# Grouped-query attention with a gated MLP on one core: next batch's transposes, the score lead, PSUM bank choice and the last batch rearranged

## The chip, the cores and the metric

One core of one Trainium2 chip. The time is device microseconds (us) of one execution, the median over runs (4 to 11 of a kernel). A profile's span is about 2 us shorter than the time of the same run.

Names: PE is TensorE (its matmuls), PEld its weight loads, ACT ScalarE, DVE VectorE, POOL GpSimd, SP SyncE (here it only issues DMAs; SPq is its queue).

Tiles in the profile lines: `sc` scores, `aT` their exps, `sums` and `X` the value products, `rec` one over the sums, `xt` the normalised X, `pv` and `v_r` the V half of the MLP, `rstd` one over its standard deviation, `v_n` V normalised, `psp` and `v_s` the spatial product, `pu` the U half, `gT` the gated product, `po` and `osb` an output tile.

## The reference, cut to what matters

Eight batches, 384 tokens. 16 query heads and 4 key/value heads of width 64 (each k/v head serves 4 query heads), then a gated MLP whose gate mixes over tokens.

```python
scores = q @ k.T / 8                        # per head, 384 x 384
attn   = exp(scores - max) / (sum + 1e-9)
x      = concat over heads of attn @ v       # (8, 384, 1024)
h      = relu(x @ w_in)                     # 1024 -> 1024
u, v   = h[..., :512], h[..., 512:]
v_n    = (v - mean) / sqrt(var + 1e-6)      # over the 512
v_s    = w_spatial @ v_n + b_spatial        # mixes the 384 tokens
out    = (u * v_s) @ w_out                  # 512 -> 1024, fp32
```

## The kernel before: the parts that matter

The kernel keeps three batches in flight. While batch `b` runs its value products (`value`: the sums of exps and two halves of X, 36 matmuls of 32-column tiles), its predecessor `c = b-1` runs the gated MLP and `d = b-2` its output. Between these blocks `more(n)` computes scores of a *later* batch, one unit (two row-tile matmuls and one exp over 128x1024) at a time, from one running list. The schedule is written by hand: each engine is given its instructions in exactly the order in which the code below emits them.

Many products are split by rows: rows 0 to 63 and rows 64 to 127 of the array work on different PSUM banks at once (`LO`, `HI`), and in a second pass they swap banks. Between the passes stands a join: a tiny memset (`mark` on POOL, `mark_v` on DVE) that waits for the first pass and that the second pass waits for.

The Trainium skill, "PSUM — Partial Sum Buffer", section "PSUM bank collisions raise a hardware error", quotes the reason for joins: different row tiles must not access the same PSUM bank at the same time.

```python
turn = [0]
def bank(shape, dtype, name, i=None):
    if i is None:
        i = turn[0]
    turn[0] = (i + 1) % 4
    return ps.tile(shape, dtype, name=name, tag=f"ps{i}")

def more(n):
    for _ in range(n):
        bu = next(ahead, None)
        if bu is not None:
            score_mm(*bu)
            exp(*bu)

def group_sp(b, banks):
    done = {}
    for m in (0, 2):
        last = pairs(sp_part(b, m, LO, banks[m]), sp_part(b, m + 1, HI, banks[m + 1]))
        done[m] = passed(last)
        if m == 0:
            more(1)
    for m in (0, 2):
        pairs(sp_part(b, m + 1, LO), sp_part(b, m, HI), after=done[m])
        sp_add(b, m)
        sp_add(b, m + 1)
        if m == 0:
            more(1)

def group_vo(bv, st, bo, i0, i1, banks, counts=(0, 2, 0), relu_on=None, then=None):
    lo = [*v_part(bv, st, LO, banks[0])]
    hi = [*o_part(bo, i0, HI, banks[1])], [*o_part(bo, i1, HI, banks[2])]
    hi = [*hi[0][:2], *hi[1][:2], *hi[0][2:], *hi[1][2:]]
    last = pairs(lo, hi, {4: [lambda: more(counts[0])]})
    done = passed(last, nc.vector)
    if then is not None:
        then()
    more(counts[1])
    pairs(
        [*o_part(bo, i0, LO), *o_part(bo, i1, LO)],
        v_part(bv, st, HI),
        {4: [lambda: o_copy(bo, i0), lambda: more(counts[2])]},
        after=done,
    )
    relu(bv, st, relu_on)
    o_copy(bo, i1)
    stats(bv, st)

def batch(b, f, o0, v, o1, late):
    c, d = b - 1, b - 2
    nxt = b + 1 < B
    value(b, 0, (f, o0, v))
    more(1)
    xmul(b, 0)
    if nxt:
        cast_all_k(b + 1)
        cast_all_q(b + 1, 0)
    group_vo(c, 2, d, 2, 3, (o1, f, o0), (late, 2, 0), nc.vector)
    if nxt:
        cast_all_q(b + 1, 1)
        cast_v(b + 1, nc.gpsimd)
        dma_transposes(b + 1)
    f, o0, v, o1 = v, f, o1, o0
    value(b, 1, (f, o0, v))
    more(1)
    rstd(c)
    xmul(b, 1)
    norm(c, 0, 2)
    group_vo(b, 0, d, 4, 5, (o1, f, o0), (late, 2, 0), then=lambda: norm(c, 2, 3))
    if b + 2 < B:
        load_all(b + 2)
    f, o0, v, o1 = v, f, o1, o0
    more(1)
    group_sp(c, (f, o0, v, o1))
    if late:
        more(1)
        group_u(c, (f, o0, v, o1))
        value(b, 2, (f, o0, v))
        more(1)
        xmul(b, 2)
    else:
        value(b, 2, (f, o0, v))
        more(1)
        xmul(b, 2)
        group_u(c, (o1, f, o0, v))
        more(2)
    if nxt:
        group_vo(b, 1, c, 0, 1, (o1, f, o0), (late, 2, late), nc.vector)
        more(1)
    return v, f, o1, o0
# (cut: loads, casts, first and second batch, tail)
```

`dma_transposes(b+1)` puts three DMA transposes (k, and q in two parts, fp16 copies made by POOL) into the SP queue. `o_copy` copies an output tile on DVE and puts its store into the same SP queue.

The softmax here doesn't subtract the row's maximum and nothing guards it: scores larger than these inputs give would overflow.

## Time and profile before

| | before |
|---|---|
| time, median | 269.22 us |
| span of the profile | 267.1 us |
| PE busy | 244.1 us, 91% |
| ACT, DVE, POOL busy | 68%, 55%, 18% |
| period of a middle batch (start of the first sums of batch 4 to that of batch 5: 128.08 to 158.19) | 30.11 us |

The page's busy line and its summary of the chain that ended last say which engine bounds the kernel:

```profile
PE 244.1 (91%) x2549; PEld 119.0 (45%) x2549; DVE 148.2 (55%) x289; ACT 181.9 (68%) x225; POOL 47.1 (18%) x100
...
PE 70%; ACT 10%; DMA 8%; DVE 6%; SPq 3%; issue 1%; ACTq 0%
```

PE bounds it, so only gaps of PE can be won. A step of 512 columns occupies 0.215 us from one start to the next (seen below); the Trainium skill, "TensorE: Matmul & The Clock Gate", section "Back-to-back issue gap", gives N/2.4 + 2.5 ns for an isolated matmul, which is 216 ns for 512 columns, and about 131 ns for a sustained stream; the trace agrees with the first and not with the second, for the sixteen full-height matmuls of two V blocks in the tail take 3.46 us in a row (241.83 to 245.29), 0.216 each. A start-to-start distance above that is lost time. The list of waits (engine, line, what it waited for, then: us in total, times, longest) names the two waits that matter:

```profile
PEld L540 <- DVE mark_v L585: 4.9, 10, 0.7
PE sc L286 <- ACT aT L297: 4.2, 11, 0.7
PE sc L286 <- DMA qT<-q: 4.1, 4, 1.6
DVE v_n L380 <- ACT rstd L373: 3.6, 7, 0.6
```

**The wait for qT.** The timeline of PE in batch 4 (start, duration, engine, line, what, in brackets the idle time ahead and its releaser):

```profile
141.26 0.38 PE L500 MATMUL pv<-w_in,xt 64*128 64x512 f16 x1
142.55 0.39 PE L286 MATMUL sc<-qT,kT 64*128 64x512 f16 x2 [0.92 <-DMA qT<-q]
```

A pair starts 0.215 us after the pair ahead of it; here 1.29 us pass from the last pair at 141.26 to the score at 142.55, so 1.1 us are lost. Over batches 3 to 6 such gaps make 4.7 us. The SP queue of the same batch shows why the data came so late:

```profile
129.29 7.17 SPq L464 DMA_DIRECT2D out_dram<-osb  x2
136.59 1.36 SPq L221 DMA_TRANSPOSE kT<-k  x1
138.07 3.35 SPq L228 DMA_TRANSPOSE qT<-q  x2
```

The row of 7.17 us merges two output stores, the second of which waits for a DVE copy until 136.1. POOL's casts, the input of the transposes, had been ready since 125.6. The first half of q landed at 142.42, and the score that needs it started at 142.55.

**The join that is late.** ACT and DVE around the group with the third output tile, same batch:

```profile
137.17 1.02 ACT L297 ACTIVATE aT<-sc 128x1024 f16<-128x1024 f32 x1 [0.35 <-PE sc L286]
138.09 0.29 ACT L372 ACTIVATE rstd<-mv,eps_t 128x3 f32<-128x3 f32 x1
138.41 0.20 ACT L373 ACTIVATE rstd<-rstd 128x3 f32<-128x3 f32 x1
```

```profile
136.86 1.29 DVE L334 TENSOR_TENSOR xt<-X,rec 128x512 f16<-128x512 f32 x2
138.65 1.47 DVE L380 TENSOR_SCALAR v_n<-v_r,mv,rstd 128x512 f16<-128x512 f32 x3 [0.50 <-ACT rstd L373]
139.59 0.06 DVE L585 MEMSET mark_v<- 1x1 f32 x1
```

The join memset at 139.59 stands behind two `v_n` on DVE, these wait for `rstd` on ACT, and `rstd` stands behind an exp. On PE, the four score matmuls ahead of the join are worth two steps, 0.43 us, but 1.03 us pass until the second pass starts:

```profile
138.70 0.79 PE L286 MATMUL sc<-qT,kT 64*128 64x512 f16 x4
139.73 0.39 PE L540 MATMUL po<-w_out,gT 64*128 64x512 f16 x1 [0.25 <-DVE mark_v L585]
```

So PE loses 0.60 us at this join, and 0.10 us at the sister group's.

**Stages.** Durations of single profiles are compared below by three stages that leave out the start-up (whose length alone varies by up to 1.5 us from profile to profile: the second sums of batch 1 start between 47.8 and 49.3 us). A: from the second sums of batch 1 to those of batch 2. B: from there to the second sums of batch 7. C: from there to the first U matmul of the tail (tile `sc_u`). All are starts read from the PE timeline of one profile for each kernel.

### The profile page before, as it was taken

Reading aid. Unit: us, or ns where it says so; the run is one execution under the profiler, and the core shown is the slowest. Engines: PE = TensorE matmul, PEld = TensorE weight load, DVE = VectorE, ACT = ScalarE, POOL = GpSimd, SP = SyncE. Lnnn points to the kernel's source line nnn. Section 1 sums busy time; section 2 is a strip of 40 time slices with the busy share of each in tenths; the row PEclk is TensorE's granted clock in tenths of the full one; section 3 lists DMA queues with packets and bytes.
Section 4 is the critical chain, followed back from the end, with each engine's and each line's share of the span. In section 5 each row is a group of like instructions: output and inputs, shape, how many; then the busy total and the mean of one; then the engine's idle time right before and its main releaser. Section 6 shows DMA issues by size and latency. Waiting matters only on the chain.

```text
span 267.1 us, 6034 instructions
## 1 busy us (share of the span) xinstructions
PE 244.1 (91%) x2549; PEld 119.0 (45%) x2549; DVE 148.2 (55%) x289; ACT 181.9 (68%) x225; POOL 47.1 (18%) x100
## 2 busy tenths in 40 slices
PE   2887988998999999799998999899999999999993
PEld 1233433553346534355444544355444544454551
DVE  2326666544276456653686356753687356757452
ACT  2889768969878696687777786687778696510501
POOL 2707803024000610007000430007000000000000
PEclk9999999999999999999999999999999999999998
DMA  8999996992269711993259801994247001210506
GB/s 185 280 260 350 271 201 85 154 312 64 81 167 277 218 66 60 198 313 107 81 137 258 267 7 77 219 320 121 81 129 179 0 20 72 103 49 0 236 2 236
DMA packets 57579, 41.68 MB, mean 156 GB/s; under 512 B 26832, under 2 KB 53840, under 8 KB 57552
## 3 DMA queue, kind: packets, MB, share of 16 engines
q1 hardware_dynamic: 53648, 37.75, 52.0%
q0 software_dynamic: 2720, 3.15, 8.4%
q10 hardware_dynamic: 1184, 0.39, 0.6%
q8 instruction: 20, 0.33, 0.5%
q14 instruction: 7, 0.06, 0.1%
HBM read 25.95 MB, written 12.58 MB: 144 GB/s over the span
## 4 chain that ended last, share of the span: by engine, by line
PE 70%; ACT 10%; DMA 8%; DVE 6%; SPq 3%; issue 1%; ACTq 0%
PE pu L513 14%; PE po L540 10%; PE sc L286 10%; PE X L307 8%; ACT aT L297 8%; DMA qT<-q 6%; PE pv L500 6%; PE sums L307 5%; PE pv L346 5%; PE psp L526 4%; PE po L442 4%; SPq L221 2%; DVE v_s L406 2%; DMA q<-in_q_dram 1%; PE pu L416 1%; DVE v_r L358 1%
## 5 line engine op out<-in xcount | busy, mean ns | idle before, releaser
L297 ACT ACTIVATE aT<-sc 128x1024 f16<-128x1024 f32 x144 | 141.0, 1023 | 41.4 <-PE sc L286 41.2
L540 PE MATMUL po<-w_out,gT 64*128 64x512 f16 x288 | 69.0, 376 | 1.7 <-DVE mark_v L585 1.2
L286 PE MATMUL sc<-qT,kT 64*128 64x512 f16 x288 | 57.1, 392 | 9.7 <-ACT aT L297 4.2
L500 PE MATMUL pv<-w_in,xt 64*128 64x512 f16 x272 | 65.8, 377 | 0.0
L513 PE MATMUL pu<-xt,w_in 64*128 64x384 f16 x448 | 41.3, 323 | 0.2 <-DVE v_s L406 0.2
L459 DVE COPY osb<-po 128x512 f32<-128x512 f32 x39 | 26.8, 689 | 22.9 <-PE po L540 19.4
L334 DVE TENSOR_TENSOR xt<-X,rec 128x512 f16<-128x512 f32 x48 | 30.9, 686 | 11.1 <-ACT rec L326 8.9
L307 PE MATMUL X<-aT,v 128*32 128x512 f16 x576 | 35.9, 384 | 0.0
L540 PEld LDWEIGHTS <-gT 64*128 64x128 f16 x288 | 25.5, 94 | 20.2 <-DVE mark_v L585 4.9
L286 PEld LDWEIGHTS <-kT 64*128 64x128 f16 x288 | 17.5, 94 | 37.3 <-issue 27.2
L428 DVE SCALAR_TENSOR_TENSOR gT<-pu,v_s 128x384 f16<-128x384 f32 x31 | 16.0, 553 | 27.4 <-PE pu L513 26.0
L513 PEld LDWEIGHTS <-w_in 64*128 64x128 f16 x448 | 24.1, 94 | 14.5 <-issue 1.4
L587 POOL MEMSET mark<- 1x1 f32 x28 | 2.5, 89 | 158.6 <-PE psp L526 116.4
L500 PEld LDWEIGHTS <-xt 64*128 64x128 f16 x272 | 24.4, 94 | 12.4 <-issue 5.5
L168 POOL CAST q<-q 128x768 f16<-128x768 f32 (+2 forms) x32 | 23.5, 770 | 27.1 <-DMA q<-in_q_dram 19.9
L406 DVE TENSOR_TENSOR v_s<-psp,bias_b 128x384 f32<-128x384 f32 x32 | 19.9, 685 | 11.2 <-PE psp L526 7.9
L307 PEld LDWEIGHTS <-v 128*32 128x32 f16 x576 | 16.5, 98 | 15.5 <-issue 1.3
L325 ACT ACTIVATE rec<-sums 128x512 f32<-128x512 f32 x24 | 14.5, 603 | 11.4 <-PE sums L307 11.4
L307 PE MATMUL sums<-aT,ones 128*32 128x512 f16 x288 | 20.6, 392 | 0.5 <-DVE v_s L406 0.3
L526 PE MATMUL psp<-wsT,v_n 64*128 64x384 f16 x168 | 17.6, 322 | 0.2 <-ACT v_r L360 0.2
L358 DVE TENSOR_SCALAR v_r<-pv 128x512 f32<-128x512 f32 x18 | 12.5, 692 | 9.0 <-PE pv L346 6.3
L367 DVE BATCH_NORM_STATS2 stats<-v_r 128x6 f32<-128x512 f32 x24 | 16.5, 690 | 0.2
(56 smaller groups left out, 154.6 us busy)
## 6 DMA issues: line engine op xcount, KB each, us to landing
out_dram<-osb SPq DMA_DIRECT2D x23, 512.0 KB, 2.9
q<-in_q_dram SPq DMA_DIRECT2D x14, 768.0 KB, 8.3
v<-in_v_dram SPq DMA_DIRECT2D x8, 384.0 KB, 8.7
k<-in_k_dram SPq DMA_DIRECT2D x7, 384.0 KB, 4.4
w_in<-in_moe_w_in_dram POOLq DMA_DIRECT2D x8, 256.0 KB, 8.9
q<-in_q_dram SPq DMA_DIRECT2D x2, 512.0 KB, 6.2
w_out<-in_moe_w_out_dram POOLq DMA_DIRECT2D x2, 512.0 KB, 20.9
ws<-in_moe_w_spatial_dram SPq DMA_DIRECT2D x1, 576.0 KB, 9.6
```

The source lines that it names most:

```text
L168: engine.tensor_copy(dst, src)
L286: mm = nc.tensor.matmul(sc[:, half, :], kT[b][lo:hi, gp, t, :], rhs[lo:hi, :], start=True, stop=True)
L297: nc.scalar.activation(aT[b, qt][:, gp, t], held["sc", b, u], AF.Exp, scale=scale)
L307: nc.tensor.matmul(dst[32 * g : 32 * (g + 1), :], weights(t, g), a[:, g // 2, t, g % 2, :], start=(t == 0), stop=(t == NST - 1),)
L334: nc.vector.tensor_tensor(xt[:, jj, :, qt * P : (qt + 1) * P], held["X", b, qt, jj].rearrange("p (j q) -> p j q", j=G), held["rec", b, qt] ...
L367: nc.vector.bn_stats(s6, held["v_r", b, st])
L406: nc.vector.tensor_tensor(held["v_s", b][:, m, :].rearrange("p (t s) -> p t s", t=NST), held["psp", b, m][:, 0:S].rearrange("p (t s) -> p ...
L459: nc.vector.tensor_copy(osb[:, cols], held["po", b, i])
L500: yield lambda kc=kc: nc.tensor.matmul(held["pv", b, st], xT[b][rows, kc, st * P : (st + 1) * P], w_in16[rows, kc, DH:DFF], start=(first a ...
L513: yield lambda kc=kc: nc.tensor.matmul(held["pu", b, mu][:, 0:S], w_in16[rows, kc, mu * P : (mu + 1) * P], xT[b][rows, kc, :], start=(firs ...
L526: yield lambda st=st: nc.tensor.matmul(held["psp", b, m][:, 0:S], held["v_n", b, st][rows, m * P : (m + 1) * P], wsT16[rows, st, :], start ...
L540: yield lambda m=m: nc.tensor.matmul(held["po", b, i], held["gT", b][rows, m, tt * P : (tt + 1) * P], w_out16[rows, m, half * 512 : (half ...
```

## The change

Its intent: (a) cast and transpose the next batch's q and k at the head of a batch, ahead of the output stores; (b) let the scores run one unit less ahead, so that the transposed data is wanted later; (c) put `rstd` ahead of the exp; (d) choose PSUM banks by least recent use; (e) in the last batch, where no scores are left to interleave, use full-height matmuls without joins for the spatial product and U, and do one V block earlier. The start of the diff (the `bank` function: a list in order of last use in place of a turning counter; default banks `None` in the groups) is cut; this is the rest:

```diff
@@ -775,24 +776,23 @@
         norm(0)
         v_full(1, 0)
         more(2)
-        group_sp(0, (0, 1, 2, 3))
+        group_sp(0)
         dma_transposes(2)
         more(1)
-        value(1, 1, (0, 1, 2))
+        value(1, 1)
         more(1)
         xmul(1, 1)
         load_all(3)
-        group_u(0, (3, 0, 1, 2))
-        more(1)
-        turn[0] = 3
+        group_u(0)
+        more(1)
         v_full(1, 1)
-        more(2)
-        value(1, 2, (0, 1, 2))
+        more(1)
+        value(1, 2)
         more(2)
         xmul(1, 2)
-        group_o(0, 0, 1, (3, 0))
+        group_o(0, 0, 1)
         more(2)
-        return 2, 1, 3, 0
+        return tuple(order)
 
     def batch(b, f, o0, v, o1, late):
 
@@ -806,16 +806,15 @@
         if nxt:
             cast_all_k(b + 1)
             cast_all_q(b + 1, 0)
-        group_vo(c, 2, d, 2, 3, (o1, f, o0), (late, 2, 0), nc.vector)
-        if nxt:
             cast_all_q(b + 1, 1)
             cast_v(b + 1, nc.gpsimd)
             dma_transposes(b + 1)
+        group_vo(c, 2, d, 2, 3, (o1, f, o0), (late, 2, 0), nc.vector)
         f, o0, v, o1 = v, f, o1, o0
 
         value(b, 1, (f, o0, v))
-        more(1)
         rstd(c)
+        more(1)
         xmul(b, 1)
         norm(c, 0, 2)
         group_vo(b, 0, d, 4, 5, (o1, f, o0), (late, 2, 0), then=lambda: norm(c, 2, 3))
@@ -823,19 +822,30 @@
             load_all(b + 2)
         f, o0, v, o1 = v, f, o1, o0
         more(1)
-        group_sp(c, (f, o0, v, o1))
         if late:
+            group_sp(c, (f, o0, v, o1))
             more(1)
             group_u(c, (f, o0, v, o1))
             value(b, 2, (f, o0, v))
             more(1)
             xmul(b, 2)
-        else:
+        elif nxt:
+            group_sp(c, (f, o0, v, o1))
             value(b, 2, (f, o0, v))
             more(1)
             xmul(b, 2)
             group_u(c, (o1, f, o0, v))
             more(2)
+        else:
+            v_full(b, 1, nc.scalar)
+            for m in range(NDT):
+                sp_mm(c, m)
+                sp_add(c, m)
+            value(b, 2)
+            xmul(b, 2)
+            for mu in range(NDT):
+                u_mm(c, mu)
+                gate(c, mu)
         if nxt:
             group_vo(b, 1, c, 0, 1, (o1, f, o0), (late, 2, late), nc.vector)
             more(1)
@@ -843,7 +853,6 @@
 
     def tail():
         c, d = B - 1, B - 2
-        v_full(c, 1)
         v_full(c, 2)
         rstd(c)
         norm(c)
```

The order of instructions on each engine, compared between the two builds, says: on SP the three transposes stand one store earlier in batches 2 to 6; POOL differs only in the last batch (four memsets fewer); DVE differs only in the last batch; on ACT one exp comes later, all through, and rstd earlier; on PE every score unit comes one place later.

More of the change, by code (lines that the diff above doesn't have):

```diff
@@ L87 @@
     )
-    turn = [0]
+    order = [0, 1, 2, 3]
     def bank(shape, dtype, name, i=None):
         if i is None:
-            i = turn[0]
-        turn[0] = (i + 1) % 4
+            i = order[0]
+        order.remove(i)
+        order.append(i)
         return ps.tile(shape, dtype, name=name, tag=f"ps{i}")
@@ L589, in passed, with group_sp @@
         return done
-    def group_sp(b, banks):
+    def group_sp(b, banks=(None,) * 4):
         done = {}
@@ L603, in group_sp, with group_u @@
                 more(1)
-    def group_u(b, banks):
+    def group_u(b, banks=(None,) * 4):
         done = {}
@@ L635, in group_vo, with group_o @@
         stats(bv, st)
-    def group_o(b, i0, i1, banks):
+    def group_o(b, i0, i1, banks=(None, None)):
         last = pairs(o_part(b, i0, LO, banks[0]), o_part(b, i1, HI, banks[1]))
@@ L813, in batch @@
             dma_transposes(b + 1)
+        group_vo(c, 2, d, 2, 3, (o1, f, o0), (late, 2, 0), nc.vector)
         f, o0, v, o1 = v, f, o1, o0
         value(b, 1, (f, o0, v))
+        rstd(c)
         more(1)
-        rstd(c)
         xmul(b, 1)
```

## The prediction

> **What bounds the kernel now.** TensorE. The page gives PE 91% of a 267.1 us span, ACT 68%, DVE 55%, POOL 18%, the granted clock full; the chain of waits is 70% PE. Useful PE time per batch (timeline spacings: 0.21 us per 512-column step, 0.16 per 384) is about 27 us, yet batches 3 to 6 repeat every 29.6 to 30.3 us. What can be won is PE idle time, which I measured from the starts of successive matmuls in the PE timeline.
>
> **Where PE idles, and what the change does.**
>
> 1. Batches 3 to 6: before the spatial group, PE waits for the DMA-transposed q of the next batch (list of waits: 4 times, 4.1 us; from starts 1.8, 1.1, 1.2, 0.6 = 4.7 us). The GpSimd casts were ready at 125.6 us, but the SP queue stood from 129.3 to 136.1 at the second output store, which waits for a DVE copy; only then came the transposes, landing near 142.4. The instruction order shows them now before that store, about 7 us earlier, and the next batch's first score one unit later. The Trainium skill, "Perfetto Trace Analysis", section "DMA Instruction — HWDGE", has the sequencer start such an instruction only once its semaphores are satisfied; this trace agrees (SP freed at 136.1). All 4.7 us should go.
>
> 2. Batches 3 to 7: in the group with the third output tile PE loses 0.60 us at a join through a tiny DVE memset (mark_v), against 0.10 in the sister group. On DVE it stands behind two v_n, which wait 0.50 us for rstd, which on ACT stands behind a 1.02 us exp. rstd now comes first: about 0.43 us each, part in batch 2; 2.4 us in all.
>
> 3. Second batch into batch 2 (58 to 78 us): ACT bound; scores wait for exp (0.4, 0.5, 0.4 us), and an exp ahead of rec delays xt and so a bank (0.55 us at 69 us). One unit fewer ahead takes one exp (0.95 us) out of this stretch: 1.2 us.
>
> 4. Last batch: row-tile pairs with joins become full-height matmuls. The spatial group took 2.8 us for 2.0 us of matmuls, U 5.45 for 5.2. The v_full is only moved (1.75 us). Gain 1.1 us. The tail from 245.3 on is dense and stays.
>
> 5. Banks by least recent use: mostly the same rotation. Near 0.
>
> **On the critical path.** All are PE gaps, so they add: 4.7 + 2.4 + 1.2 + 1.1 = 9.4 us. ACT (22.3 us per 30) and DVE (17.6) have room. Start-up (about 11 us idle) and small joins stay.
>
> **Prediction: 259.8 us, range 257.8 to 262.5. Chances: faster by over 2% 0.94, within 2% 0.055, slower 0.005.**
>
> **What would show it.** Period of batches 3 to 6 near 28.5 us (from about 30.1). (1) No PE wait for qT; transposes about 7 us earlier, before the second store. (2) DVE's wait for rstd near 0, loss at that join near 0.2 us. (3) PE's waits for exp around 60 to 66 us mostly gone. (4) End of batch 7's second group to the tail's first output matmul (231.3 to 245.3, 14.0 us) about 0.9 us shorter although one score unit has joined it.
>
> **What would make it wrong.** Casts not ready at the new place, so that transposes hold the stores; without the qT wait, the spatial group may wait for relu on ACT or the output copy on DVE, hidden so far under it (0.2 to 0.4 us per batch); rstd before exp may delay scores; the ACT-bound stretch may not shorten; in the last batch the spatial product may wait for banks.

## More of the kernel before

All runs quoted are of the fast state with a granted TensorE clock of 0.996 to 1.0.

Before: A 25.29, B 151.11, C 25.77 us, together 202.17.

## The result, and the profile after

| | before | after |
|---|---|---|
| time, median (range) | 269.22 us (268.73 to 269.54) | 261.19 us (260.78 to 261.48) |
| ratio, 95% interval | | 0.9702 (0.9682 to 0.9722) |
| span | 267.1 us | 259.3 us |
| period, batch 4 to 5 | 30.11 us | 28.60 us |
| stages A, B, C | 25.29, 151.11, 25.77 us | 24.70, 144.60, 24.93 us |

A ratio here is the mean time of one kernel's fast runs over that of the other's of the same rounds, so it is not quite the ratio of the medians. The stages give 202.17 - 194.23 = 7.9 us, the spans 7.8 us. The page of the changed kernel:

```profile
PE 242.2 (93%) x2505; PEld 125.0 (48%) x2505; DVE 147.5 (57%) x288; ACT 182.1 (70%) x226; POOL 46.6 (18%) x96
...
PE 84%; ACT 8%; DVE 4%; DMA 1%; issue 1%; ACTq 0%
```

The chain is now PE for 84%; the shares of DMA and of the SP queue have gone. In its list of waits no line for DMA qT is left:

```profile
PE sc L287 <- ACT aT L298: 4.2, 11, 0.7
...
PEld L541 <- DVE mark_v L586: 2.3, 10, 0.2
...
DVE v_n L381 <- ACT rstd L374: 0.6, 1, 0.6
```

The SP queue in batch 4 (which starts at 125.32 in this profile, 2.76 us sooner than in the other):

```profile
126.53 0.36 SPq L465 DMA_DIRECT2D out_dram<-osb  x1
126.98 1.41 SPq L222 DMA_TRANSPOSE kT<-k  x1
128.53 4.59 SPq L229 DMA_TRANSPOSE qT<-q  x2
133.64 5.81 SPq L465 DMA_DIRECT2D out_dram<-osb  x2
```

The first transpose is issued 126.98 - 125.32 = 1.7 us into the batch; before it was 136.59 - 128.08 = 8.5 us. The first half of q lands at 133.74, 4.5 us before its score. PE runs through where it waited:

```profile
138.07 0.38 PE L501 MATMUL pv<-w_in,xt 64*128 64x512 f16 x1
138.20 0.47 PE L287 MATMUL sc<-qT,kT 64*128 64x512 f16 x2
138.42 0.74 PE L527 MATMUL psp<-wsT,v_n 64*128 64x384 f16 x6
```

ACT and DVE at the join: `rstd` precedes the exp, DVE goes from `xt` to `v_n` without a pause, and the memset comes 136.35 - 125.32 = 11.03 us into the batch (before: 11.51).

```profile
134.17 0.30 ACT L373 ACTIVATE rstd<-mv,eps_t 128x3 f32<-128x3 f32 x1
134.50 0.20 ACT L374 ACTIVATE rstd<-rstd 128x3 f32<-128x3 f32 x1
134.61 1.01 ACT L298 ACTIVATE aT<-sc 128x1024 f16<-128x1024 f32 x1
```

```profile
134.10 1.29 DVE L335 TENSOR_TENSOR xt<-X,rec 128x512 f16<-128x512 f32 x2
135.30 1.58 DVE L381 TENSOR_SCALAR v_n<-v_r,mv,rstd 128x512 f16<-128x512 f32 x3
136.35 0.06 DVE L586 MEMSET mark_v<- 1x1 f32 x1
```

PE now passes the join in 0.52 us, so 0.09 us are lost in place of 0.60:

```profile
135.94 0.79 PE L287 MATMUL sc<-qT,kT 64*128 64x512 f16 x4
136.46 0.39 PE L541 MATMUL po<-w_out,gT 64*128 64x512 f16 x1
```

### The profile page after: what moved, and what is told of

It is laid out like the page before. It is cut to its first block, busy times and chain, and to the rows that moved or that the text cites. A ratio compares the mean times of both kernels' runs of the same rounds, so it can differ in the third digit from the quotient of the medians.

```text
span 259.3 us, 5937 instructions
## 1 busy us (share of the span) xinstructions
PE 242.2 (93%) x2505; PEld 125.0 (48%) x2505; DVE 147.5 (57%) x288; ACT 182.1 (70%) x226; POOL 46.6 (18%) x96
## 4 chain that ended last, share of the span: by engine, by line
PE 84%; ACT 8%; DVE 4%; DMA 1%; issue 1%; ACTq 0%
PE po L541 15%; PE pu L514 12%; PE sc L287 12%; PE X L308 11%; PE pv L501 9%; PE sums L308 7%; ACT aT L298 6%; PE pv L347 5%; PE po L443 4%; PE pu L417 4%; PE psp L527 3%; DVE v_s L407 2%; DMA q<-in_q_dram 1%; DVE xt L335 1%; PE psp L395 1%; ACT rec L327 1%
## 5 line engine op out<-in xcount | busy, mean ns | idle before, releaser
L287 PE MATMUL sc<-qT,kT 64*128 64x512 f16 x288 | 58.1, 392 | 5.6 <-ACT aT L298 4.2
L514 PE MATMUL pu<-xt,w_in 64*128 64x384 f16 x384 | 35.8, 322 | 0.2 <-DVE v_s L407 0.2
L287 PEld LDWEIGHTS <-kT 64*128 64x128 f16 x288 | 18.4, 94 | 31.0 <-issue 21.1
L514 PEld LDWEIGHTS <-w_in 64*128 64x128 f16 x384 | 20.8, 94 | 12.2 <-issue 0.7
L359 DVE TENSOR_SCALAR v_r<-pv 128x512 f32<-128x512 f32 x17 | 11.8, 691 | 9.3 <-PE pv L347 6.7
L327 ACT ACTIVATE rec<-rec 128x512 f32<-128x512 f32 x24 | 15.1, 630 | 0.8
```

Of the source, the lines that this page charges most:

```text
L287: mm = nc.tensor.matmul(sc[:, half, :], kT[b][lo:hi, gp, t, :], rhs[lo:hi, :], start=True, stop=True)
L327: nc.scalar.activation(r, r, AF.Exp, scale=-1.0)
L514: yield lambda kc=kc: nc.tensor.matmul(held["pu", b, mu][:, 0:S], w_in16[rows, kc, mu * P : (mu + 1) * P], xT[b][rows, kc, :], start=(firs ...
```

## The experiments

All gave correct results. Ratios are to the kernel before. The stages settle differences under 1 us, which the times alone cannot.

| run | time, us | ratio (95%) | A | B | C |
|---|---|---|---|---|---|
| before | 269.22 | 1 | 25.29 | 151.11 | 25.77 |
| after | 261.19 | 0.9702 (0.9682 to 0.9722) | 24.70 | 144.60 | 24.93 |
| e1_transposes_first | 264.93 | 0.9839 (0.9811 to 0.9867) | 25.30 | 146.41 | 25.76 |
| e2_rstd_first | 268.46 | 0.9977 (0.9951 to 1.0002) | 25.29 | 151.27 | 25.26 |
| e3_both | 262.23 | 0.9737 (0.9710 to 0.9765) | 25.24 | 144.56 | 25.27 |
| e4_unit_back | 261.99 | 0.9733 (0.9705 to 0.9761) | 25.24 | 144.59 | 24.72 |
| f1_stats_later | 260.55 | 0.9693 (0.9675 to 0.9710) | 24.65 | 144.58 | 24.63 |
| f2_tile_by_tile | 257.59 | 0.9579 (0.9565 to 0.9594) | 23.99 | 142.00 | 24.76 |
| f3_unit_elsewhere | 260.64 | 0.9691 (0.9675 to 0.9706) | 24.33 | 144.57 | 24.94 |
| f4_all_three | 257.73 | 0.9573 (0.9550 to 0.9596) | 23.88 | 141.99 | 24.47 |
| g1_last_batch_old | 261.19 | 0.9706 (0.9682 to 0.9730) | 24.65 | 144.59 | 25.27 |
| g2_banks_only | 269.06 | 0.9994 (0.9972 to 1.0015) | 25.30 | 151.03 | 25.77 |
| g3_two | 257.58 | 0.9567 (0.9542 to 0.9592) | 24.05 | 142.00 | 24.46 |
| g4_other_half_first | 266.42 | 0.9892 (0.9867 to 0.9917) | 25.14 | 148.89 | 25.36 |

### e1_transposes_first: one part alone, the SP order

On the kernel before, in `batch`:

```diff
             cast_all_q(b + 1, 0)
-        group_vo(c, 2, d, 2, 3, (o1, f, o0), (late, 2, 0), nc.vector)
-        if nxt:
             cast_all_q(b + 1, 1)
             cast_v(b + 1, nc.gpsimd)
             dma_transposes(b + 1)
+        group_vo(c, 2, d, 2, 3, (o1, f, o0), (late, 2, 0), nc.vector)
```

> The kernel before with one part of the change: the casts of the second q half and of v, and the three DMA transposes, stand ahead of the first group of a batch; nothing else. Theory A (the SP queue stood behind the second output store, and that alone made TensorE wait for qT): the four waits of TensorE for qT (4.7 us by starts) go wholly, time about 4.7 us below before (264.5 us), the joins behind mark_v still lose 0.60 us each. Rival B (the transposes are needed so soon that the unit less ahead is wanted as well): some wait for qT stays, gain under 4 us. Rival C (the casts or the transposes themselves are late): gain under 1 us.

Measured: B fell by 151.11 - 146.41 = 4.70 us, A and C did not move, and no wait for qT is left. Theory A holds to the tenth. The unit less ahead was not needed for it (rival B falls), and neither casts nor transposes were late in themselves (rival C falls): POOL's order is the same in both kernels. The time says 4.3 us (ratio 0.9839); in the profiled run the start-up was 1.0 us longer than before (49.31 against 48.30), in the other runs it was not measured.

### e2_rstd_first: one part alone, the join

```diff
-        more(1)
         rstd(c)
+        more(1)
         xmul(b, 1)
```

> The kernel before with one part of the change: rstd stands before the score unit and its exp. Theory A (the gaps of TensorE add, as the prediction says): about 2.2 to 2.5 us below before. Rival B (in batches 3 to 6 the landing of qT is set by the copy of the second output tile, which comes before this join, so a join that ends 0.5 us sooner only waits 0.5 us longer for qT): the gain is seen in batches 2 and 7 only, 0.4 to 0.9 us, and TensorE's waits for qT grow by about 0.5 us each, from 4.1 to about 6 us.

Measured: ratio 0.9977, an interval that reaches 1; B 0.16 us *longer*, C 0.51 shorter. DVE's wait for rstd is gone (3.6 to 0.6 us), and PE's wait for qT has grown from 4.1 us, as the first line of PE's waits in this run shows:

```profile
PE sc L286 <- DMA qT<-q: 6.0, 4, 2.0
```

Rival B holds. In batches 3 to 6 the join lies between two events that it does not move: the copy of the second output tile, which frees the SP queue, and the landing of qT. A join 0.5 us sooner only starts the next wait 0.5 us sooner. The gain shows only in batch 7, which has no next batch to transpose.

### e3_both

The two edits together.

> Both parts, transposes first and rstd first, on the kernel before. Theory A and rival B both: 4.7 + 2.5 = about 7 us below before (262.2 us); under rival B the sum is larger than the two parts measured alone by about 2 us. If it is nearer to the sum of the parts alone under B's numbers (5.3 us), the join's gain is lost elsewhere.

Measured: A + B + C = 195.07 us, 7.10 below before. Alone, the parts gave 4.70 and 0.35. The 2.05 us that are missing from the sum of the parts are the join's gain in batches 3 to 6, which appears only once the wait behind it is gone.

### e4_unit_back: the unit of lead

On the changed kernel, in the second batch:

```diff
         v_full(1, 1)
-        more(1)
+        more(2)
         value(1, 2)
```

> The changed kernel with the one unit put back (two units after the second v_full of the second batch, as before). Theory: the unit's move is worth little, because ScalarE then idles about 0.5 us of the 0.95 us at the place, and 0.21 us of TensorE work is only moved into the last batch: about 0.2 to 0.5 us above the changed kernel (261.4 to 261.7 us). Rival (the prediction's figure): 1.2 us above. No wait for qT comes back in either.

Measured: A 25.24, as in e3 and 0.54 above the changed kernel; C 0.21 below it, which is the one score unit (one 512-column step) that is no longer done in the last batch. Net 0.32 us, not 1.2. No wait for qT came back. The lists of waits name PE's wait for exp with 4.2 us, 11 times, before and after, but these are sums over the whole run, and the start-up is part of them. In stage A the waits are three before (0.42, 0.52 and 0.36 us, 1.3 us together) and two after (0.52 and 0.36, 0.9 us). ACT in this stretch, before and after (cut to the first reciprocal of batch 2):

```profile
60.95 0.60 ACT L325 ACTIVATE rec<-sums 128x512 f32<-128x512 f32 x1
...
62.12 5.58 ACT L297 ACTIVATE aT<-sc 128x1024 f16<-128x1024 f32 x6
67.54 0.64 ACT L325 ACTIVATE rec<-sums 128x512 f32<-128x512 f32 x1
```

```profile
60.16 0.59 ACT L326 ACTIVATE rec<-sums 128x512 f32<-128x512 f32 x1
...
61.62 5.61 ACT L298 ACTIVATE aT<-sc 128x1024 f16<-128x1024 f32 x6 [0.21 <-PE sc L287]
67.06 0.65 ACT L326 ACTIVATE rec<-sums 128x512 f32<-128x512 f32 x1
```

Counted from the start of stage A (48.30 and 48.42), the earlier reciprocal comes 12.65 - 11.74 = 0.91 us sooner: one exp fewer stands ahead of it. Then ACT idles 0.21 us for a score that comes only behind a whole value product (0.5 us were expected), where in the kernel before the exp follows without a pause, and the first reciprocal of batch 2 comes only 19.24 - 18.64 = 0.60 us sooner.

### f1_stats_later: why the last batch gave less

On the changed kernel, in the last batch:

```diff
-            v_full(b, 1, nc.scalar)
+            v_mm(b, 1)
+            relu(b, 1, nc.scalar)
             for m in range(NDT):
                 sp_mm(c, m)
                 sp_add(c, m)
+            stats(b, 1)
             value(b, 2)
```

> The changed kernel; in the last batch the statistics of the V block (second of three) come after the four v_s additions on VectorE, not ahead. Theory (the full-height last batch gave 0.55 us and not 1.1 because VectorE's v_s stood behind these statistics, which wait for relu on ScalarE, and the sums wait 0.4 us for a bank that v_s reads): the wait of sums before the last value product goes, the stretch from the second sums of batch 7 to the tail's U (24.93 us) gets 0.4 us shorter, about 260.8 us. Rival (PE's switch between matmul shapes costs it): no change.

In the changed kernel, DVE in the last batch:

```profile
226.97 0.70 DVE L368 BATCH_NORM_STATS2 stats<-v_r 128x6 f32<-128x512 f32 x1 [1.14 <-ACT v_r L361]
...
227.79 2.49 DVE L407 TENSOR_TENSOR v_s<-psp,bias_b 128x384 f32<-128x384 f32 x4
```

The v_s additions stand behind statistics that wait for relu, and the sums, which take the bank of the first spatial product, wait for them (0.23 us of idle shown, 0.40 us by starts). A wait of this size is not new: from the last spatial matmul to the sums 0.59 us pass in the kernel before, where v_s waited for the second pass, 0.56 in the changed kernel and 0.26 with this edit. With the statistics behind, C fell from 24.93 to 24.63 us and the wait of the sums is gone from the list. Theory right for this wait, 0.30 us against 0.4 expected; the time's interval overlaps the changed kernel's, so the stage decides this. The rival is not nothing either: in e4 0.31 us pass from the last half-array matmul to the first full-height one, where in e3 the next half-array matmul follows after 0.13. The two kernels' last batches then add up: spatial product 0.49 us shorter, U 0.24 shorter, this switch 0.18 longer, together the 0.55 us by which their C differ.

### f2_tile_by_tile: the gap at the third step

On the changed kernel, in `group_vo`:

```diff
-        hi = [*hi[0][:2], *hi[1][:2], *hi[0][2:], *hi[1][2:]]
+        if i0:
+            hi = [*hi[0], *hi[1]]
+        else:
+            hi = [*hi[0][:2], *hi[1][:2], *hi[0][2:], *hi[1][2:]]
```

> The changed kernel; in the groups with output tiles 1 and 2 the first pass does all four steps of one output half before the other, so the half whose bank the xt multiplication frees comes 0.43 us later. Theory (TensorE's loss at the third step, 0.56 and 0.40 us in batches 2 and 3, 0.23 in 4 to 7 against a base of 0.1, is the wait for that bank): these go, 1.0 to 1.2 us in all, about 260.1 us. Rival (in batch 2 ScalarE's row of exps bounds the stretch): only 0.5 to 0.7 us.

Measured: A + B + C fell by 194.23 - 190.75 = 3.5 us and the ratio to 0.9579. The direction was right and the size was three times too small. In the changed kernel, PE's timeline at the head of the first group of batch 4 and at its end:

```profile
128.04 0.38 PE L501 MATMUL pv<-w_in,xt 64*128 64x512 f16 x1
128.38 0.37 PE L541 MATMUL po<-w_out,gT 64*128 64x512 f16 x1
128.39 0.39 PE L501 MATMUL pv<-w_in,xt 64*128 64x512 f16 x1
...
129.46 0.38 PE L541 MATMUL po<-w_out,gT 64*128 64x512 f16 x1
129.48 0.79 PE L287 MATMUL sc<-qT,kT 64*128 64x512 f16 x4
130.01 0.39 PE L541 MATMUL po<-w_out,gT 64*128 64x512 f16 x1
130.10 0.38 PE L501 MATMUL pv<-w_in,xt 64*128 64x512 f16 x1
```

At the third step the V matmul starts at 128.04 but its partner starts only at 128.38. It writes the bank that the first `xt` multiplication has to leave: that instruction starts at 127.64 and takes 0.69 us. The next V matmul has a bank that is free, and yet it starts behind the late partner. The Trainium skill, "TensorE: Matmul & The Clock Gate", section "The mechanism" of Part 3, says that matmuls start and end in program order ("strict FIFO, no reordering"), and these starts agree. The wait is 128.38 - 128.04 - 0.215 = 0.13 us, which is what I had counted. But from here on the row streams are one step apart. The output stream ends with a matmul whose partner is a score and not a V matmul (129.46), and the second pass starts its halves 0.09 us apart. With the new order the pair of the third step starts together, 0.215 us after the second:

```profile
126.22 0.38 PE L501 MATMUL pv<-w_in,xt 64*128 64x512 f16 x1
126.22 0.38 PE L541 MATMUL po<-w_out,gT 64*128 64x512 f16 x1
```

From the first to the second sums of batch 4 this kernel takes 6.26 us, the changed one 6.60: 0.34 us for a wait of 0.13. In the second group of the same batch the partner is only 0.20 us late (V matmul at 134.64, partner at 134.84, next V matmul at 134.85), so no step of V is lost there, and yet the new order gives 0.16 us (9.19 to 9.03). That the step apart itself costs the rest is read from these starts; it was not varied alone.

### g4_other_half_first: the same cause, made larger

```diff
         if i0:
-            hi = [*hi[0], *hi[1]]
+            hi = [*hi[1], *hi[0]]
```

> The changed kernel; in the groups with output tiles 1 and 2 the output half whose bank the xt multiplication frees comes first, so its bank is wanted at the first step and not at the third. Theory (TensorE takes its matmuls in order, so the wait for that bank holds the V steps too and puts the two row streams out of step): the wait grows by about 0.43 us in the first group of batches 2 to 7 and appears in the second, 3 to 6 us above the changed kernel (264 to 267 us), with TensorE waiting for DVE xt. Rival (the gain of the half-by-half order comes from the order of the outputs in itself, such as fewer switches of bank): the same 3.5 us below the changed kernel as the other half-by-half order.

Measured: 266.42 us, 5.2 us above the changed kernel. The stretch from the first to the second sums of batch 4 takes 7.03 us against 6.60, so +0.43, two steps, as computed; the next one (to the third sums) 9.62 against 9.19, again +0.43. PE's wait for xt, one time and 0.3 us in the changed kernel, heads the list:

```profile
PE po L541 <- DVE xt L335: 4.4, 12, 0.7
```

The rival falls: doing one half after the other is only good if the half with the free bank goes first.

### f3_unit_elsewhere

On the changed kernel, in the second batch:

```diff
         v_full(1, 1)
-        more(1)
+        more(2)
         value(1, 2)
...
         group_o(0, 0, 1)
-        more(2)
+        more(1)
```

> The changed kernel; the unit that it drops ahead of the value product in the second batch is put back there, and one is dropped at the end of the second batch. Theory (the drop was worth 0.3 us and not 1.2 because ScalarE then waits about 0.5 us for a score behind that value product): the number of exps before the first reciprocal of batch 2 is the same, ScalarE stays fed, and the body gets 0.3 to 0.5 us shorter, about 260.8 us. Rival (where the unit is dropped does not matter): the same as the changed kernel, 261.2 us.

Measured: A 24.33 against 24.70, B and C the same. The idle time of ACT ahead of this row is gone. From 59 us on, as many exps stand ahead of the first reciprocal of batch 2 as in the changed kernel, seven (before: eight); here they are two and then five, there one and then six:

```profile
61.91 4.66 ACT L298 ACTIVATE aT<-sc 128x1024 f16<-128x1024 f32 x5
66.43 0.63 ACT L326 ACTIVATE rec<-sums 128x512 f32<-128x512 f32 x1
```

That reciprocal comes 66.43 - 48.14 = 18.29 us into the stage, 0.95 us sooner than before, a whole exp. The place where the unit is dropped is worth 0.37 us in A, beside 0.54 for the drop. In time the two kernels are not told apart (the intervals overlap); the stage is the evidence.

### f4_all_three and g3_two: versions that beat both kernels

f4 has the edits of f1, f2 and f3; g3 those of f1 and f2.

> All three of these edits on the changed kernel. If they add: 0.4 + 1.1 + 0.4 = 1.9 us below the changed kernel, 259.3 us. The second and third touch the same stretch of batch 2, so some 0.3 us may be counted twice: 259.3 to 259.8 us.

> The changed kernel with two of the follow-up edits, output half by half and statistics later, without the unit moved elsewhere. If the unit's place is worth nothing beside them: as the version with all three, 257.3 to 257.7 us; else 0.3 us above it.

Measured: 257.73 and 257.58 us, ratios 0.9573 and 0.9567 to before, not told apart from each other nor from f2 alone (0.9579). The stage sums are 190.34, 190.51 and 190.75 us, against 194.23 of the changed kernel. Beside f2, f3 is worth 24.05 - 23.88 = 0.17 us in A and not 0.37: both shorten the same waits of batch 2. f4 came out below its expected 259.3 to 259.8 because f2 was mis-sized.

### g1_last_batch_old

The changed kernel with the last batch and the tail as before (the lines of the last `else` in the diff undone).

> The changed kernel with the last batch as before (row-tile pairs with joins for the spatial product and U, both V blocks in the tail). Theory (the full-height last batch is worth 0.55 us net, as the comparison of two runs said): about 0.5 to 0.6 us above the changed kernel, 261.7 us, all of it between the second sums of batch 7 and the tail's U. Rival (the prediction's figure): 1.1 us above.

Measured: the time is that of the changed kernel (261.19 us; ratios 0.9706 and 0.9702), and C is 0.34 us longer. Both theories fall (0.5 to 0.6 us, and 1.1): my 0.55 came from e3 against e4, which is 0.55 with the old lead. In g1 the spatial group takes 226.50 - 223.88 = 2.62 us, before it took 234.32 - 231.49 = 2.83: the score unit that is now left for the last batch stands ahead of the group and hides the relu that the group waited for. So what the full-height last batch is worth depends on the lead: 0.55 us without the moved unit, 0.34 with it.

### g2_banks_only

The choice of banks alone on the kernel before.

> The kernel before with the choice of PSUM banks by least recent use alone (second batch and what follows from it). Theory: within 0.2 us of before, 269.2 us, as the later batches name their banks. Rival (the rotation of banks was part of the gain): 0.5 us or more below.

Measured: ratio 0.9994; the stages agree within 0.1 us. The choice of banks in itself is worth nothing on the kernel before; in the rearranged last batch, where the new code leaves the choice to it, it was not tested apart.

## Why the prediction was right, point by point

The prediction was 259.8 us with 257.8 to 262.5; the time is 261.19, in the range. It forecast 9.4 us and 8.0 came (269.22 - 261.19). The two large terms (1 and 2) carry it: 7.10 us of the 7.1 forecast (e3). The two small ones (3 and 4) gave 0.84 us of 2.3.

1. *The wait for qT, "All 4.7 us should go"*: right, 4.70 us (e1). The cause, the second store in the SP queue, was tested alone.
2. *The join, "2.4 us in all"*: right in the whole, 195.07 - 197.47 = -2.40 us (e3 against e1). Wrong in the sentence behind it, "All are PE gaps, so they add": alone it brings 0.35 us (e2). The sum came out since the change removes both.
3. *"One unit fewer ahead takes one exp (0.95 us) out of this stretch: 1.2 us"*: the term of the sum that was most mis-sized. It measured 0.54 us in stage A, of which 0.21 us is work moved to the last batch (e4). The exp did leave the stretch, but ACT then idled for a score, so the first reciprocal of batch 2 came 0.60 us sooner and not 0.95; with ACT kept fed it came 0.95 sooner, and A fell by another 0.37 us (f3). The sign "PE's waits for exp around 60 to 66 us mostly gone" did not come: 1.3 us before, 0.9 after. The loss at 69 us, where PE waits for xt, stayed too (0.67 us from start to start in both kernels).
4. *Last batch, "Gain 1.1 us"*: mis-sized, 0.34 to 0.55 us (g1; e3 against e4). I took the full gap of 2.8 against 2.0 us in the spatial group as won. Half of it, a wait of the sums for v_s of 0.40 us, stayed, now behind the statistics (f1 removes 0.30 of it); 0.18 us went to the switch to full-height matmuls; and part was a wait for relu that the moved score unit hides anyway (g1). U gave 0.24 us of the 0.25 expected. The sign, 0.9 us off the 14.0 from batch 7's second group to the tail's first output matmul, came as 0.4 (231.28 to 245.29 before, 223.87 to 237.47 after).
5. *Banks, "Near 0"*: right (g2).

Taken in order from before: transposes and rstd 7.10 (e3), last batch and banks 0.52 (e4 against e3), unit 0.32 (after against e4); together 7.94 us, the whole difference of the stages. Period of batch 4: 28.60 us, predicted near 28.5. None of the feared counter-effects in batches 3 to 6 appeared: B of the changed kernel is 6.5 us shorter, 4.7 + 1.85 as the two parts give.

Left open: that ACT's idle time is what the drop by one unit lost is shown by the starts on ACT and by f3, but why even with ACT fed A fell by 0.91 us (25.24 in e4 to 24.33) and not by 1.2 was not looked into. f2 was not run on the kernel before, so how much of its 3.5 us would have been hidden behind the wait for qT is not known.

## What to carry to other kernels

In this kernel the DMA queue was a queue of waits: put what the critical engine will need ahead of stores that wait for something late, and check with the instruction order that it stands there. Gaps on one engine add only if no later event in the same period has its own fixed time; test a small gain again once the large wait behind it is gone. When two half-array streams run in pairs, order each stream so that its first steps write banks that are already free: the wait itself was 0.13 us and cost 0.34.

## What the Trainium skill lacked or had wrong

- "TensorE: Matmul & The Clock Gate", Part 3: it has the strict program order of matmuls, but not what that does to two row-tile streams. A wait of 0.13 us in one put them a step apart until the end of the group and cost 0.34 us together (f2); moving the wanted bank two steps earlier cost 0.43 us more per group (g4).
- "DMA: Bandwidth & Descriptors", section "Latency and other measured facts": it gives 261 GB/s for a DMA transpose with a non-contiguous middle dimension and 350 to 400 GB/s for a contiguous one. Here three of them (k and two of q, fp16, 0.98 MB together) took 7.2 us from the first issue at 136.59 to the last landing at 143.81, an estimate of 136 GB/s that holds other traffic and the time between the issues. No page gives for trn2 what one of these sizes holds its issuing queue for: in batch 4 1.36 us (before) and 1.41 (after) for the 128x768 k, 1.33 and 1.49 (before), 1.43 and 3.05 (after) for the two of 128x1536; why one took twice as long is open.
- "Perfetto Trace Analysis", section "DMA Instruction — HWDGE": it shows the semaphore wait ahead of the profiled time of one DMA, and the sequencer free for the next instruction only at its end, but does not draw what follows for those behind it. Here a store that waited to 136.1 kept transposes whose input was ready at 125.6, and 4.7 us of TensorE time hung on it.
